# Moving layer 2's sums from GpSimd to VectorE, and s and b from the weights to the activations

## The chip, the core and the metric

The kernel runs on one core of a Trainium2 chip. A core has five engines with a queue each: TensorE (PE, with its weight load PEld), VectorE (DVE), ScalarE (ACT), GpSimd (POOL) and SyncE (SP, which here issues the DMAs). The metric is the device time of one execution in microseconds (us). Before the change it is 1638.78 us, the median of three runs (1637.3 to 1640.04).

## The reference

Linear attention feeds two dense layers. What is computed, cut to the arithmetic:

```python
kv  = einsum('bhsd,bhse->bhde', k, v)             # 8 batches, 8 heads, 576 rows, 64 wide
out = einsum('bhsd,bhde->bhse', q, kv)
x   = out / sqrt(mean(out*out, -1) + 1e-6) * g_norm   # as 4608 tokens x 512

h = x @ w_in1;  g = h * sigmoid(1.702 * h);  x = g @ w_out1     # 512 -> 2048 -> 512
h = x @ w_in2;  r = max(h, 0);  g = s * (r * r) + b;  out = g @ w_out2
```

s and b are one number each. All inputs are float32; the weights come as 64-bit words that the kernel turns into float32 itself.

## The kernel before, in words

Every float32 factor is split into a high part, rounded for TensorE, and the low rest. A product is then three matmuls: high x high, low x high, high x low. ACT makes the high part (a copy with rounding, `CAST`), DVE the low one (a subtraction).

The tokens come in 9 blocks of 512. The first three blocks of layer 1 run as plain matmuls (`mm1`, `mm2`). From there two blocks make a *couple*, and products of 2 x 2 block matrices are done with 7 block products instead of 8. Couples 0 to 2 are layer 1 (blocks 3 to 8), couples 3 to 6 are layer 2 (blocks 0 to 7), couple 7 is the *narrow* one (block 8, 256 wide). A couple has 8 *pairs*, one for 2 x 128 of the 2048 hidden columns, and a pair has 7 steps. One step of one pair is called a *slot* here.

In each slot `product` (L672) puts 6 matmuls of 512 columns on TensorE. Their right side is `xs[s, i]` (tiles `wi0` to `wi6`), one of 7 sums of the couple's input blocks, made by `y_get` (L502: load the four blocks into tiles `f0` to `f3`, and add up partial sums where layer 1 stored several), `fac_sums` (L530: three sums) and `split_x` (L544: high and low part, a fourth sum for i = 6). `after` (L768) takes the products from PSUM: ACT copies, DVE adds, ACT applies the activation. In layer 2 that is `Relu` and then `Square` (`sq`, L736).

In layer 2 two pairs make a *quad*, 14 slots. The activations of a quad, tiles `raws` e0 to e3, are the factors of 7 further products M1, M4, M7, M5, M6, M2, M3: M1, M4 and M2 use e0, e1 and e3 as they are, the other four need a sum of e's. `factor_add` (L923) makes that sum (tile `s`), on GpSimd; `factor_hi` (L945, ACT) and `factor_lo` (L953, DVE) split it (tile `fac`). `quad_unit` (L960) then puts 12 matmuls of 256 columns on TensorE, one half-product per slot, in the slots of the next quad. The three lines L979, L980 and L981 are high x high, high x low weights, and low x high, so the low part is first needed by the third matmul. M2 and M3 stay in PSUM over a couple (tile `msum`); the others are added into SBUF (tile `madd`) by DVE, or copied by ACT in a couple's first quad.

When a couple's M's are complete, `combine` (L1000) adds them to the four output blocks, per half h: five sums of SBUF tiles on GpSimd (L1012), two with PSUM on DVE, and four DMAs out.

s and b in layer 2: `prep_out` (L279) makes the 8 combinations of each weight pair and `scaled_hl` (L266) multiplies them by s while it splits them. For b, GpSimd adds all weight tiles up in `col0` (L285 to L289); `make_bias` (L865) multiplies that with b by one matmul, and the result is added when M1 and M5 of a couple are first stored (L988), and at the end of the narrow couple (L918).

What sets the order: every engine runs its queue in order. The main loop (L1520) writes, per slot, the product, what `after` does with the last one, the factors (`factors`, L1501: sums 4 slots ahead of their use, splits 2 ahead), a unit of the quad before, and then as much of the list of background tasks (`background`, L1225) as is due or fits: the kernel keeps a rough count of DVE's and ACT's time (`clock`), and lets a task go on while the larger count is under the slot's limit. Tasks are `y_get`, `fac_sums`, `split_x`, `combine`, and the conversion of layer 2's weights (`convert2`, `prepare2`), which runs during layer 1's couples. What runs on GpSimd isn't counted.

Of the kernel before, what the change touches and what calls it, by code (L numbers as in the profile page):

```python
# [44 lines left out]
SLACK2 = 0.6  # L45
# [7 lines left out]
def tile_attn_moe_moe2(  # L53
# [210 lines left out]
    wt_dram, column = {}, [None]  # L264

    def scaled_hl(dst, src, n):  # L266

        yield
        yield from spaced()
        t = rot("wst", 2, (P, 2, 2, KP), F32R)[:, 0:n]  # L270
        scalar.activation(out=t[:, :, 0, :], in_=src, func=ACTF.Copy, scale=s_sb[:, 0:1])
        yield 1
        vector.scalar_tensor_tensor(
            out=t[:, :, 1, :], in0=src, scalar=s_sb[:, 0:1], in1=t[:, :, 0, :].bitcast(F32),
            op0=ALU.mult, op1=ALU.subtract,
        )
        move(dst, t)

    def prep_out(p):  # L279

        wa, wb = (w_raw.pop((1, 1, f)) for f in (2 * p, 2 * p + 1))
        add = nc.gpsimd.tensor_tensor
        if p == 0:
            column[0] = new("col0")
            add(out=column[0], in0=wa, in1=wb, op=ALU.add)  # L285
            wt_dram.update({x: dp.tile([P, 8, 2, 2, KP], F32, name=f"wt{x}") for x in range(KF // 4)})
        else:
            add(out=column[0], in0=column[0], in1=wa, op=ALU.add)
            add(out=column[0], in0=column[0], in1=wb, op=ALU.add)  # L289
# [478 lines left out]
    def after(P_, i):  # L768
# [20 lines left out]
        elif i == 5:  # L789
            c = c_t[P_, 2]  # L790
            tt(out=c, in0=take(P_, "D"), in1=c, **add)
            sq(P_, 1)
            act(P_, 2)
        else:
            c_new(P_, 3)
            act(P_, 3, take(P_, "A"))
            g_hi(P_, 1)
            g_lo(P_, 1)
            sq(P_, 2)
            sq(P_, 3)  # L800
# [61 lines left out]
    t_t, f_t, mid_t, m_ps, m_sb, bias = {}, {}, {}, {}, {}, {}  # L862
    t_next = [0]

    def make_bias():  # L865

        b_all = kvbd[0][:, 0, :]
        o = bank("a1", "bias")
        nc.tensor.matmul(o, b_all, column[0], start=True, stop=True)
        t = new("ev1", name="bias")  # L870
        scalar.copy(t, o)
        d = new("g0", (P, KP), name="biasd")
        vector.tensor_tensor(out=d, in0=t[:, KP:2 * KP], in1=t[:, 0:KP], op=ALU.subtract)
        bias[0], bias[1], bias["all"] = t[:, 0:KP], d, t
# [36 lines left out]
    def narrow_out(t, c):  # L911
# [5 lines left out]
        for lo, hi in zip(cuts, cuts[1:]):  # L917
            vector.tensor_tensor(out=e[:, lo:hi], in0=o[:, lo:hi], in1=bias["all"][:, lo:hi], op=ALU.add)  # L918
# [4 lines left out]
    def factor_add(q_, k_):  # L923
# [3 lines left out]
        tt = nc.gpsimd.tensor_tensor  # L927
# [32 lines left out]
    def quad_unit(q_, k_, h):  # L960
# [21 lines left out]
        if not held(q_, k_):  # L982
            if first:
                a = m_sb[key] = new(ADD_PLACE[10 + h if k_ == M1 and s % 2 else 2 * k_ + h], (P, 2, KP), name="madd")
                if k_ not in (M1, M5):
                    scalar.copy(a, o)
                else:
                    more = bias[k_ == M5].rearrange("p (o d) -> p o d", o=1).to_broadcast([P, 2, KP])  # L988
                    vector.tensor_tensor(out=a, in0=o, in1=more, op=ALU.add)
# [10 lines left out]
    def combine(s, h):  # L1000
# [9 lines left out]
        def plus(k_, more, psum=False):  # L1010
# [3 lines left out]
        while (s, M6, h) not in ended:  # L1014
            yield 1
        plus(M6, m_sb[s, M1, h])
        plus(M7, m_sb[s, M6, h])
        plus(M6, m_sb[s, M5, h])
        plus(M5, m_sb[s, M7, h])
        plus(M7, m_sb[s, M4, h])  # L1020
        while (s, M2, h) not in ended:
            yield 1
        plus(M1, m_ps[s, M2, h], True)
        yield 1
        send(M1, 0, 0)
        yield 1
        send(M5, 1, 1)
        yield 1
        send(M7, 1, 0)
        while (s, M3, h) not in ended:  # L1030
            yield 1
        plus(M6, m_ps[s, M3, h], True)
# [167 lines left out]
    def plan():  # L1200
# [3 lines left out]
        for s_ in range(len(couples)):  # L1204
            n0 = n * s_
            need = []
            if s_:
                if couples[s_][0]:
                    need = [Task(y_get(s_), n0 - n + 6, n0 - n + 7)]
                need = [Task(fac_sums(s_), n0 - 14, n0 - 9, need)]  # L1210
            for i in range(7):
                if (s_, i) in split_early:
                    continue
                more = [split[s_, 1]] if (i == 6 and (s_, 1) in split) else []
                split[s_, i] = Task(split_x(s_, i), max(0, n0 - 7 + i + 1), max(0, n0 + i - (3 if i < 6 else 5)), need + more)
# [9 lines left out]
    def background(tick, slot, share):  # L1225

        limit = (tick + share) * slot
        ready = [t for t in tasks if t.ready <= tick and all(x.done for x in t.behind)]
        for t in sorted(ready, key=lambda t: due(t, tick)):
            while not t.done and t.ready <= tick and (due(t, tick) <= tick or max(clock.values()) < limit):  # L1230
                t.step(tick)

    with tc.manual_schedule():
# [286 lines left out]
        for P_, (s_, p) in enumerate(pairs):  # L1520
            lay, m, js = couples[s_]
            short = m < BT
            for i in range(7):
# [23 lines left out]
                for _ in range(2 if i == 6 else 1):  # L1547
# [9 lines left out]
                background(tick, slot, SLACK2 if lay and not short else SLACK)  # L1557
# [62 lines left out]
```

## Time and profile before

One profiled execution took 1639.39 us; its span, from the first to the last instruction, is 1637.5 us, at a mean granted TensorE clock of 0.992.

| engine | busy us | share of the span | instructions |
|---|---|---|---|
| PE (matmul) | 1579.5 | 96% | 9026 |
| PEld (weight load) | 1352.1 | 83% | 9026 |
| DVE | 984.5 | 60% | 1398 |
| ACT | 832.4 | 51% | 1430 |
| POOL | 403.3 | 25% | 208 |

The page's slices show TensorE busy at 90% or more nearly everywhere; layer 1's couples run from about 337 us, layer 2 from about 875 us, the narrow couple's own part from about 1560 us. A busy TensorE is one with matmuls in its pipe; how long it stood still, and for whom, is read from the view of waits. A wait is put down to the engine whose signal came last. Busy time of DVE or POOL is the time from an instruction's start to its end, also where it stood still inside.

### The profile page before, as it was taken

How to read it: one execution, taken by the hardware profiler on the slowest of the kernel's cores; microseconds unless marked ns; L12 is line 12 of the kernel's file. 1: busy time of each engine (PE TensorE's matmuls, PEld its weight loads, DVE VectorE, ACT ScalarE, POOL GpSimd, SP SyncE). 2: the span in 40 equal slices, each digit the busy share in tenths (PEclk: the TensorE clock that was granted, in tenths of full speed). 3: DMA queues.
4: the chain of work that ended last, by engine and by line, in shares of the span. 5: the costliest groups of instructions: out<-in, count | busy, mean ns of one | idle time of the engine just before them, and what ended most of it. 6: DMA issues, size and time to landing. Idle time of an engine off the chain costs nothing.

```text
span 1637.5 us, 23547 instructions
## 1 busy us (share of the span) xinstructions
PE 1579.5 (96%) x9026; PEld 1352.1 (83%) x9026; DVE 984.5 (60%) x1398; ACT 832.4 (51%) x1430; POOL 403.3 (25%) x208
## 2 busy tenths in 40 slices
PE   8999999999989999999889999999999999999899
PEld 7888878878877787888768898889888988899887
DVE  6777643456577667686875345754575457545732
ACT  4765633454545544554335645554555455554543
POOL 4000111101130113001440224442445244523410
PEclk9999999999999999999999999999999999999999
DMA  8678776567757766689765655575557555755584
GB/s 270 214 267 295 283 257 228 211 217 258 239 190 265 258 225 231 231 328 331 285 212 195 245 192 179 181 269 187 181 180 268 190 180 177 249 192 191 195 296 164
DMA packets 126434, 376.95 MB, mean 230 GB/s; under 512 B 12530, under 2 KB 30194, under 8 KB 118130
## 3 DMA queue, kind: packets, MB, share of 16 engines
q1 hardware_dynamic: 126178, 375.31, 66.9%
q8 instruction: 72, 1.18, 0.3%
q14 instruction: 40, 0.33, 0.1%
q10 hardware_dynamic: 144, 0.13, 0.0%
HBM read 295.70 MB, written 79.69 MB: 229 GB/s over the span
## 4 chain that ended last, share of the span: by engine, by line
PE 78%; DVE 11%; issue 4%; POOL 3%; DMA 2%; ACT 2%; SPq 0%; DVEq 0%; POOLq 0%; ACTq 0%
PE A L686 6%; PE A L687 5%; PE A L688 5%; PE m L981 4%; PE m L980 4%; PE m L979 4%; PE D L686 3%; PE D L687 3%; PE D L688 3%; DVE fac L89 3%; PE acc L626 2%; PE acc L627 2%; PE acc L628 2%; PE h L598 2%; PE h L600 2%
## 5 line engine op out<-in xcount | busy, mean ns | idle before, releaser
L981 PE MATMUL m<-wo,fac 128*128 128x256 f32 x640 | 183.0, 286 | 15.1 <-DVE fac L89 15.1
L440 POOL TENSOR_TENSOR r<-ms,mhalf 128x8 f32<-128x8 f32 x36 | 66.0, 1837 | 488.6 <-DVE ms L89 488.5
L980 PE MATMUL m<-wo,fac 128*128 128x256 f32 x640 | 181.2, 283 | 0.0
L979 PE MATMUL m<-wo,fac 128*128 128x256 f32 x640 | 180.5, 282 | 0.1
L89 DVE TENSOR_TENSOR madd<-m,madd 128x512 f32<-128x512 f32 x120 | 82.5, 687 | 101.4 <-PE m L981 101.4
L686 PE MATMUL A<-wi,xl 128*128 128x512 f32 (+1 forms) x340 | 131.5, 387 | 11.7 <-ACT ev L89 5.7
L981 PEld LDWEIGHTS m<-wo,fac 128*128 128x128 f32 x640 | 121.6, 190 | 18.3 <-DVE fac L89 17.9
L89 ACT ACTIVATE gh<-gh 128x512 f32<-128x512 f32 x72 | 45.4, 631 | 170.8 <-DVE gh L89 170.6
L687 PE MATMUL A<-wi,xl 128*128 128x512 f32 (+1 forms) x340 | 129.6, 381 | 0.0
L688 PE MATMUL A<-wi,xl 128*128 128x512 f32 (+1 forms) x340 | 128.6, 378 | 0.0
L979 PEld LDWEIGHTS m<-wo,fac 128*128 128x128 f32 x640 | 121.8, 190 | 6.9 <-issue 0.3
L980 PEld LDWEIGHTS m<-wo,fac 128*128 128x128 f32 x640 | 122.4, 191 | 5.8
L89 ACT ACTIVATE wraw<-wraw 128x512 uint32<-128x512 uint32 (+1 forms) x128 | 83.0, 648 | 80.8 <-DVE wraw L89 80.5
L89 DVE TENSOR_TENSOR fac<-s,fac 128x1024 fp32r<-128x1024 f32 x64 | 84.3, 1318 | 8.9 <-ACT fac L89 8.9
L686 PEld LDWEIGHTS A<-wi,xl 128*128 128x128 f32 x340 | 64.6, 190 | 24.0 <-ACT ev L89 6.5
L828 PE MATMUL z<-wo,wo 128*128 128x512 f32 x192 | 77.3, 403 | 5.9 <-DVE g L89 5.8
L89 DVE TENSOR_TENSOR wi<-f,wi 128x1024 fp32r<-128x1024 f32 (+1 forms) x56 | 73.9, 1327 | 9.3 <-ACT wi L89 9.3
L89 ACT ACTIVATE wi<-wi 128x512 f32<-128x512 f32 x64 | 40.5, 632 | 73.2 <-DVE wi L89 73.0
L598 PE MATMUL h<-xh,wi 128*128 128x512 f32 x192 | 76.5, 398 | 1.2 <-ACT g L89 1.2
L626 PE MATMUL acc<-gh,wo 128*128 128x512 f32 x192 | 76.7, 399 | 0.0
L627 PE MATMUL acc<-gh,wo 128*128 128x512 f32 x192 | 75.1, 391 | 1.1 <-DVE wo L89 1.1
L829 PE MATMUL z<-wo,wo 128*128 128x512 f32 x192 | 75.6, 394 | 0.0
(251 smaller groups left out, 4589.9 us busy)
## 6 DMA issues: line engine op xcount, KB each, us to landing
wo<-wt SPq DMA_DIRECT2D x127, 512.0 KB, 3.7
xl<-wi SPq DMA_DIRECT2D x42, 1024.0 KB, 6.6
wo<-wo SPq DMA_DIRECT2D x80, 512.0 KB, 5.3
xl<-wi SPq DMA_DIRECT2D x43, 768.0 KB, 5.8
xh<-wi SPq DMA_DIRECT2D x22, 1024.0 KB, 6.8
wi<-wst SPq DMA_DIRECT2D x40, 512.0 KB, 4.8
wraw<-in_w_in SPq DMA_DIRECT2D x32, 512.0 KB, 4.6
wraw<-in_w_out SPq DMA_DIRECT2D x32, 512.0 KB, 4.4
```

The costliest lines, as they stand in the source:

```text
L89: return fn(*args, **kw)
L598: nc.tensor.matmul(o, wh[:, cs], xh[:, c, :], start=(c == 0), stop=False)
L626: nc.tensor.matmul(o, wh[:, ds_], gh, start=(f == lo), stop=False)
L627: nc.tensor.matmul(o, wl[:, ds_], gh, start=False, stop=False)
L686: nc.tensor.matmul(o, wh, xh, start=(c == 0 and not more), stop=False, skip_group_check=more)
L687: nc.tensor.matmul(o, wl, xh, start=False, stop=False, skip_group_check=more)
L688: nc.tensor.matmul(o, wh, xl, start=False, stop=(c == 1), skip_group_check=more)
L828: nc.tensor.matmul(o, wh[:, cs], gh, start=begins, stop=False)
L829: nc.tensor.matmul(o, wl[:, cs], gh, start=False, stop=False)
L979: nc.tensor.matmul(o[:, c, :], hi[:, y, cs], w[:, y, 0, :], start=begins, stop=False)
L980: nc.tensor.matmul(o[:, c, :], hi[:, y, cs], w[:, y, 1, :], start=False, stop=False)
L981: nc.tensor.matmul(o[:, c, :], lo[:, y, cs], w[:, y, 0, :], start=False, stop=ends)
```

## The change

Five things change.

1. `fac_sums`, the fourth sum of `split_x`, `factor_add` and the five SBUF sums of `combine` run on DVE. For layer 2's couples after the first, `fac_sums` also makes the fourth sum, into tiles of its own, and it may start 35 slots ahead instead of 14. The adds in `y_get` and the power in `att_r` (L440) stay on GpSimd.
2. `prep_out` splits the weights unscaled (`parts_hl` for `scaled_hl`); the column sum, `make_bias` and the adds of the bias are gone. Instead `sq` is followed by a second ACT instruction on each activation tile, `Identity` with scale s and bias b.
3. `sq` of layer 2's wide couples is put on a list and issued after the slot's factors; the one of e3 is moved into the next pair's first slot, that of e1 in every second pair to the last slot of the pair.
4. In a couple's first quad M1 and M5 are copied by ACT like the others. `combine` may start 6 slots earlier, its sums are spread over slots, and the last wide couple has an order of its own (M3 copied out of PSUM by ACT first).
5. The background list has one limit for both layers (0.9 of a slot instead of 0.6 in layer 2), and in layer 2 a second one: a slot's tasks may add 500 ns to DVE's count. The units of layer 1's last pair are spread over more slots, and the two factor tile pairs change places.

```diff
-    def prep_out(p): ... add = nc.gpsimd.tensor_tensor; add(out=column[0], ...)
-        yield from scaled_hl(d[:, 0:8:7], a, 2)
+        yield from parts_hl(d[:, 0:8:7], a, 2)
...
     def fac_sums(s):
-        tt = (nc.gpsimd if s else vector).tensor_tensor
+        tt = vector.tensor_tensor
...
+        if s > first2:
+            fac[s, 6] = [new(tag, (P, couples[s][1]), name="f6") for tag in ("ev1", "g0")]
+            for c in range(2):
+                tt(out=fac[s, 6][c], in0=b21[:, c, :], in1=t2[:, c, :], op=ALU.subtract)
+                yield 1
...
+    late = []
+    def sq(P_, e, now_=False):
+        if layer(P_) and not narrow(P_) and not now_:
+            late.append((P_, e))
+        elif layer(P_):
             c = c_t[P_, e]
             scalar.activation(out=c, in_=c, func=ACTF.Square)
+            scalar.activation(out=c, in_=c, func=ACTF.Identity, scale=s_sb[:, 0:1], bias=b_sb[:, 0:1])
...
     def factor_add(q_, k_):
-        tt = nc.gpsimd.tensor_tensor
+        tt = vector.tensor_tensor
...
-                if k_ not in (M1, M5):
-                    scalar.copy(a, o)
-                else:
-                    more = bias[k_ == M5].rearrange("p (o d) -> p o d", o=1).to_broadcast([P, 2, KP])
-                    vector.tensor_tensor(out=a, in0=o, in1=more, op=ALU.add)
+                scalar.copy(a, o)
...
     def combine(s, h):
-            (vector if psum else nc.gpsimd).tensor_tensor(out=a, in0=more, in1=a, op=ALU.add)
+            vector.tensor_tensor(out=a, in0=more, in1=a, op=ALU.add)
...
                 if lay:
                     factors(*at_q)
+                if i == 0 and P_ > P2 and not narrow(P_ - 1):
+                    sq(P_ - 1, 3)
+                while late:
+                    sq(*late.pop(0), True)
...
-                background(tick, slot, SLACK2 if lay and not short else SLACK)
+                background(tick, slot, SLACK, ROOM if lay and P_ > P2 + 1 else 9999.0)
```

How the instructions stand. First GpSimd, from the last adds of `y_get` to the first sums of layer 2; `f` are the couple's input tiles, `col` the column sum, `s` the sums of activations. Before:

```order
L522 TENSOR_TENSOR f_6552<-f_6552,f_7354 128x1024
L528 TENSOR_TENSOR f_6552<-f_6552,f_7405 128x1024
L288 TENSOR_TENSOR col_3842<-col_3842,wf 128x512
L289 TENSOR_TENSOR col_3842<-col_3842,wf 128x512
L535 TENSOR_TENSOR f_7541<-f_6551,f_6549 128x1024
L537 TENSOR_TENSOR f_7542<-f_6552,f_7541 128x1024
L539 TENSOR_TENSOR f_6551<-f_6552,f_6551 128x1024
L548 TENSOR_TENSOR f_6550<-f_6550,f_7542 128x1024
L930 TENSOR_TENSOR s_7991<-wraw_7739,wst_7773 128x1024
L933 TENSOR_TENSOR s_8047<-wst_7773,wraw_7798 128x1024
```

Now the same engine, with the new file's line numbers (L503 and L509 are `y_get`):

```order
L503 TENSOR_TENSOR f_6538<-f_6538,f_7232 128x1024
L503 TENSOR_TENSOR f_6539<-f_6539,f_7286 128x1024
L503 TENSOR_TENSOR f_6539<-f_6539,f_7339 128x1024
L509 TENSOR_TENSOR f_6539<-f_6539,f_7390 128x1024
L1624 UNCONDITIONAL_BRANCH
```

Only the adds of `y_get` are left there; behind them the queue is empty to the end of the program.

Next VectorE, where couple 6 begins, from the first unit's add on; `wi` are the low parts of the couple's new right sides, `fac` the low parts of the factors, `wraw` and `wst` the activations. Before:

```order
L89 TENSOR_TENSOR madd<-m,madd 128x512
L89 TENSOR_TENSOR wi_10645<-f_10299,wi_10645 128x1024
L89 TENSOR_TENSOR wraw_10656<-B,wraw_10656 128x512
L89 TENSOR_TENSOR fac<-wi_10277,fac 128x1024
L89 TENSOR_TENSOR madd<-m,madd 128x512
L89 TENSOR_TENSOR wi_10678<-f_10298,wi_10678 128x1024
L89 TENSOR_TENSOR madd<-m,madd 128x512
L89 TENSOR_TENSOR wi_10707<-f_9343,wi_10707 128x1024
L89 TENSOR_TENSOR fac<-s_10658,fac 128x1024
```

Now:

```order
L89 TENSOR_TENSOR s_10708<-wi_10321,xh_10376 128x1024
L89 TENSOR_TENSOR madd<-m,madd 128x512
L89 TENSOR_TENSOR wi_10695<-f_9770,wi_10695 128x1024
L89 TENSOR_TENSOR wraw_10706<-B,wraw_10706 128x512
L89 TENSOR_TENSOR fac<-wi_10321,fac 128x1024
L89 TENSOR_TENSOR madd<-m,madd 128x512
L89 TENSOR_TENSOR wi_10730<-f_9332,wi_10730 128x1024
L89 TENSOR_TENSOR s_10772<-xh_10376,wi_10321 128x1024
L89 TENSOR_TENSOR madd<-m,madd 128x512
L89 TENSOR_TENSOR wi_10759<-f_9333,wi_10759 128x1024
L89 TENSOR_TENSOR wi_10761<-f_9855,wi_10761 128x512
L89 TENSOR_TENSOR fac<-s_10708,fac 128x1024
```

The two sums `s` of M7 and M5 now stand in DVE's queue, ahead of adds that free PSUM and ahead of the low parts that the next products need.

Last ScalarE at the same place, `CAST` being the high parts, `COPY` the products taken from PSUM. Before:

```order
L89 ACTIVATE xh_10333<-A 128x512
L89 ACTIVATE xh_10333<-xh_10333 128x512 x2
L89 CAST wi_10645<-f_10299 128x1024
L89 COPY wraw_10656<-A 128x512
L89 CAST fac<-wi_10277 128x1024
L89 CAST wi_10678<-f_10298 128x1024
L89 ACTIVATE wraw_10656<-wraw_10656 128x512
```

Now, with `Identity` as the rows that read `b_sb,s_sb`:

```order
L89 ACTIVATE xh_10376<-A 128x512
L89 ACTIVATE wi_10321<-wi_10321 128x512
L89 ACTIVATE wi_10321<-wi_10321,b_sb,s_sb 128x512
L89 ACTIVATE xh_10376<-xh_10376 128x512
L89 ACTIVATE xh_10376<-xh_10376,b_sb,s_sb 128x512
L89 CAST wi_10695<-f_9770 128x1024
L89 COPY wraw_10706<-A 128x512
L89 CAST fac<-wi_10321 128x1024
L89 ACTIVATE xh_10376<-xh_10376 128x512
L89 ACTIVATE xh_10376<-xh_10376,b_sb,s_sb 128x512
L89 CAST wi_10730<-f_9332 128x1024
L89 ACTIVATE wraw_10706<-wraw_10706 128x512
```

Three squares and three `Identity` stand between the last pair's final `Relu` and the high part of the new right sides; before it were two squares.

## Rows read from the trace of the kernel before

**Rows 1.** Waits of PE: who for whom: us in total, times, longest

```profile
PE m L981 <- DVE fac L89: 15.1, 14, 2.2
PE z L828 <- DVE g L89: 5.8, 4, 4.3
PE A L686 <- ACT ev L89: 5.7, 2, 4.7
PE D L686 <- DVE gh L89: 4.6, 1, 4.6
PE xtp L450 <- DVE xn L89: 4.3, 4, 2.1
PE A L686 <- DVE gh L89: 2.3, 2, 1.9
PE D L688 <- DVE wi L89: 2.0, 2, 1.4
```

**Rows 2.** Timeline in layer 2: start us, us, engine, line, what [idle before]

```profile
1242.30 2.38 POOL L933 TENSOR_TENSOR s<-wst,wraw 128x1024 f32<-128x1024 f32 x1
...
1242.39 3.37 DVE L89 TENSOR_TENSOR fac<-wraw,fac 128x1024 fp32r<-128x1024 f32 x1
...
1246.59 1.22 DVE L89 TENSOR_TENSOR fac<-s,fac 128x1024 fp32r<-128x1024 f32 x1 [0.23 <-ACT fac L89]
...
1245.82 0.39 PE L981 MATMUL m<-wo,fac 128*128 128x256 f32 x1 [1.11 <-DVE fac L89]
```

**Rows 3.** Timeline late in layer 1: GpSimd, and what TensorE waited for

```profile
780.44 1.74 POOL L288 TENSOR_TENSOR col<-col,wf 128x512 f32<-128x512 f32 x1
782.25 1.62 POOL L289 TENSOR_TENSOR col<-col,wf 128x512 f32<-128x512 f32 x1
783.84 2.81 POOL L522 TENSOR_TENSOR f<-f,f 128x1024 f32<-128x1024 f32 x1
...
844.99 2.46 POOL L537 TENSOR_TENSOR f<-f,f 128x1024 f32<-128x1024 f32 x1
...
842.69 2.51 DVE L89 TENSOR_TENSOR wc<-wf,wc 128x256 f32<-128x256 f32 x1
...
852.01 0.74 PE L686 MATMUL A<-wi,xl 128*128 128x512 f32 x1 [4.66 <-ACT ev L89]
```

**Rows 4.** Windows: us, busy of PE, PEld, DVE, ACT, POOL, granted clock, DMA share, GB/s

```profile
473.20:480.10 6.90, 5.78 (x14) 4.52 (x15) 4.46 (x9) 0.43 (x1) 0.00 (x0) 0.51 0.61 194
790.60:794.10 3.50, 3.50 (x10) 2.73 (x9) 3.50 (x3) 2.46 (x5) 2.47 (x1) 0.51 0.38 150
852.10:855.60 3.50, 3.50 (x9) 2.73 (x10) 2.56 (x4) 2.62 (x5) 0.00 (x0) 0.51 0.75 243
1039.80:1043.30 3.50, 3.50 (x13) 2.88 (x12) 3.12 (x4) 1.20 (x3) 0.23 (x1) 0.51 0.02 5
1203.60:1207.10 3.50, 3.50 (x14) 3.01 (x13) 3.20 (x4) 1.10 (x2) 0.00 (x0) 0.51 0.00 0
```

**Rows 5.** Groups by shape: busy us, mean ns of one, idle before

```profile
L89 DVE TENSOR_TENSOR f<-f,f 128x1024 f32<-128x1024 f32 x4 | 4.8, 1221 | 2.9 <-ACT f L89 2.8
L89 DVE TENSOR_TENSOR madd<-m,madd 128x512 f32<-128x512 f32 x120 | 82.5, 687 | 101.4 <-PE m L981 101.4
L1012 POOL TENSOR_TENSOR madd<-madd 128x512 f32<-128x512 f32 x40 | 61.9, 1551 | 24.3 <-DVE madd L89 21.8
L936 POOL TENSOR_TENSOR s<-s,wraw 128x1024 f32<-128x1024 f32 x8 | 19.2, 2400 | 33.7 <-DVE fac L89 33.7
L89 DVE TENSOR_TENSOR fac<-s,fac 128x1024 fp32r<-128x1024 f32 x64 | 84.3, 1318 | 8.9 <-ACT fac L89 8.9
L89 ACT CAST fac<-s 128x1024 fp32r<-128x1024 f32 x64 | 66.6, 1040 | 0.0
L89 ACT CAST wi<-wf 128x512 fp32r<-128x512 f32 x16 | 9.9, 619 | 4.7 <-DVE wf L89 4.7
L89 ACT ACTIVATE wst<-wf,s_sb 128x512 fp32r<-128x512 f32 x16 | 11.5, 719 | 0.0
```

**Rows 6.** Timeline of TensorE: the first matmul of two slots that follow each other

```profile
1249.94 0.40 PE L686 MATMUL A<-wi,xl 128*128 128x512 f32 x1
...
1252.74 0.40 PE L686 MATMUL D<-wi,xl 128*128 128x512 f32 x1
```

**Rows 7.** Windows as in rows 4: a quad within a couple, and one where a couple begins

```profile
1280.00:1320.00 40.00, 40.00 (x260) 36.42 (x259) 19.15 (x23) 20.03 (x31) 10.21 (x6) 1.00 0.58 189
1360.00:1400.00 40.00, 37.54 (x239) 33.47 (x238) 30.26 (x29) 20.78 (x30) 23.05 (x13) 1.00 0.62 206
```

More of the change, by code (lines that the diff above doesn't have):

```diff
@@ L44 @@
 SLACK = 0.9
-SLACK2 = 0.6
+ROOM = 500.0
 W_LEAST = 2.0 ** -15
@@ L791, in after @@
             tt(out=c, in0=take(P_, "D"), in1=c, **add)
-            sq(P_, 1)
+            if not (layer(P_) and not narrow(P_) and P_ % 2):
+                sq(P_, 1)
             act(P_, 2)
@@ L796, in after @@
             act(P_, 3, take(P_, "A"))
+            if layer(P_) and not narrow(P_) and P_ % 2:
+                sq(P_, 1)
             g_hi(P_, 1)
@@ L861, in tile_attn_moe_moe2 @@
     quads = [(s_, x) for s_ in range(first2, len(couples) - 1) for x in range(KF // 2 // BY)]
-    t_t, f_t, mid_t, m_ps, m_sb, bias = {}, {}, {}, {}, {}, {}
+    t_t, f_t, mid_t, m_ps, m_sb = {}, {}, {}, {}, {}
     t_next = [0]
[L865 to L874, printed above, removed]
     def load_t():
@@ L917, in narrow_out @@
         for lo, hi in zip(cuts, cuts[1:]):
-            vector.tensor_tensor(out=e[:, lo:hi], in0=o[:, lo:hi], in1=bias["all"][:, lo:hi], op=ALU.add)
+            (vector.tensor_copy if lo else scalar.copy)(e[:, lo:hi], o[:, lo:hi])
             (nc.scalar if hi < DM else nc.sync).dma_start(out=out[row:row + P, lo:hi], in_=e[:, lo:hi])
@@ L1008, in send, with plus, until @@
             nc.sync.dma_start(out=dst, in_=m_sb[s, k_, h])
-        def plus(k_, more, psum=False):
+        def plus(k_, more):
             a = m_sb[s, k_, h]
-            (vector if psum else nc.gpsimd).tensor_tensor(out=a, in0=more, in1=a, op=ALU.add)
-        while (s, M6, h) not in ended:
-            yield 1
[L1016 to L1023, printed above, removed]
+            vector.tensor_tensor(out=a, in0=more, in1=a, op=ALU.add)
+        def until(k_):
+            while (s, k_, h) not in ended:
+                yield 1
+        sums = ((M7, M6), (M6, M5), (M5, M7), (M7, M4))
+        plus(M6, m_sb[s, M1, h])
+        if s == len(couples) - 2:
+            yield from until(M2)
+            plus(M1, m_ps[s, M2, h])
+            yield from until(M3)
+            last = new(f"f{h}", (P, 2, KP), name="m3")
+            scalar.copy(last, m_ps[s, M3, h])
+            yield 4
+            send(M1, 0, 0)
+            for k_, e in sums:
+                plus(k_, m_sb[s, e, h])
+                yield 2
+            send(M5, 1, 1)
+            plus(M6, last)
+            yield 2
+            send(M7, 1, 0)
+            yield 2
+            send(M6, 0, 1)
+            return
+        yield from until(M6)
+        for k_, e in sums:
+            plus(k_, m_sb[s, e, h])
+            yield 1
+        send(M5, 1, 1)
+        yield from until(M2)
+        plus(M1, m_ps[s, M2, h])
+        yield 1
+        send(M7, 1, 0)
         yield 1
         send(M1, 0, 0)
[L1026 to L1032, printed above, removed]
+        yield from until(M3)
+        plus(M6, m_ps[s, M3, h])
         yield 1
@@ L1128, in tiles_in @@
             at((P_, 3 * e + 3), "pre", x_raw, i + e)
-    for x, slot in ((0, 2), (0, 2), (0, 5), (0, 5), (1, 3)):
+    for x, slot in ((0, 2), (0, 2), (0, 5), (0, 5), (1, 5)):
         at((P2 + x, slot), "load", load_t)
-    b_all = kvbd[0][:, 0, :]
-    at((P2, 3), "pre", lambda: scalar.activation(out=b_all, in_=ident, func=ACTF.Identity, scale=0.0, bias=b_sb[:, 0:1]))
-    at((P2 + 1, 3), "post", make_bias)
     at(n0 + 10, "load", load_q, 5 * TT)
@@ L1223, in due, with background @@
         return task.deadline() if callable(task.deadline) else task.deadline
[L1225 removed]
+    def background(tick, slot, share, room):
         limit = (tick + share) * slot
+        most = clock["dve"] + room
         ready = [t for t in tasks if t.ready <= tick and all(x.done for x in t.behind)]
         for t in sorted(ready, key=lambda t: due(t, tick)):
[L1230 removed]
+            while not t.done and t.ready <= tick and (due(t, tick) <= tick or (max(clock.values()) < limit and clock["dve"] < most)):
                 t.step(tick)
```

59 lines of the change are left out of this document (25 added, 34 removed), and 2 rows, old and new, of the table PLACES.

## The prediction

> **What bounds the kernel now.** I read the page's busy shares first: TensorE has matmuls in its pipe for 96% of the span, so time can come only from the moments in which it stands still or is clocked low. So the view of waits comes next, cut to PE's own [rows 1]. In layer 2 it waits 15.1 us for low parts of factors, mostly where a couple begins, and 2.0 us for low parts of right sides. In layer 1 it waits 5.8 us for g, 5.7 for ev, 4.6 and 2.3 for gh, 4.3 for xn: 22.7 us. Each is a tile that VectorE or ScalarE delivers late, yet both are free about half the time [rows 7]. Why late?
>
> The timeline answers. One and the same subtraction takes 3.37 us while a GpSimd sum of 2.38 us runs, and 1.22 us four microseconds later with GpSimd idle; TensorE's 1.11 us wait stands behind it [rows 2]. Late in layer 1 a 128x256 subtraction takes 2.51 us and ends at 845.2, just after GpSimd has gone over from one sum to the next (844.99), and the delay arrives at TensorE as 4.66 us [rows 3]. A VectorE instruction with two SBUF inputs thus seems to stand still until GpSimd's sum ends.
>
> Then the windows by clock: after five of the long waits the granted clock is 0.51 for 6.90 or 3.50 us, that is the lower level of 1.2 GHz [rows 4]. About half of each window is lost: 6.90 x 0.49 + 2 x 3.50 x 0.49 = 6.8 us in layer 1, 2 x 3.50 x 0.49 = 3.4 us in layer 2.
>
> **What is removed.** GpSimd loses 64 factor sums of some 2.4 us, 40 output sums of 1.55 us [rows 5], the 26 or so sums of `fac_sums` and `split_x` (2.46 us, a half for the narrow couple) and 15 column adds (1.74 and 1.62 us in the two that I show) [rows 3]. It keeps the adds of `y_get`, one of which took 2.81 us [rows 3]. In layer 2 nothing is left that could hold VectorE up.
>
> [...]
>
> **What is added, VectorE.** 64 sums at 1.22 us (the same shape and operands from SBUF: 1221 ns) are 78 us over 16 quads; 40 output sums at 0.69 us, taken like the 687 ns of `madd` with one PSUM input, are 27 us [rows 5]. A quad lasts 14 slots of 2.80 us, the distance between two slots' first matmuls [rows 6], or 39.2 us. Within a couple VectorE was busy 19.15 of 40 us [rows 7]; four sums add 4.9: about 24, far from full. Where a couple begins it was busy 30.26 [rows 7], of which about 5 was standing still beside GpSimd's 23.05 us; with 4.9 of factor sums, 3 of `fac_sums` and some output sums it comes to 30 to 34. It stays below the slot rate, but an engine that full in a queue delivers late now and then. In the narrow couple's first 11 or so slots I count 26 to 27 us of VectorE's work in about 23.5 us of matmuls: there it is the bound for a short while.
>
> **What is added, ScalarE.** Eight `Identity` per quad. The trace has none with two pointer operands: a copy is 619 ns, one with a pointer scale 719 ns [rows 5]. From below 0.62, from above 0.92 (three such steps of 100 ns); I take 0.82, the one step doubled. That is 6.6 us per quad on top of 20.03 of 40 us, or 20.78 where a couple begins [rows 7], plus two copies for M1 and M5 in a first quad: 27 to 28 of 39.2 us. At 0.92 it is 0.8 us more per quad, nothing while the queue has gaps.
>
> The first wait where that load counts is the sum of M7 in a couple's first slots, e0 - e2. Call the start of the old couple's last slot 0. The `Identity` of e2 ends at about 4.6. Before the `CAST` of the sum the ScalarE queue then holds four `CAST` at 1.04, two halves at 0.62, two copies and a `Relu` and a square at about 0.62, and one `Identity` at 0.82: 4.2 + 1.2 + 2.5 + 0.8 = 8.7 (lengths from [rows 5]; the shapes that it doesn't show are taken as the copy's). With its own 1.04 it ends at 14.3, and the subtraction of 1.32 [rows 5] at 15.6, or up to 17.0 if VectorE's queue has a low part and an add ahead of it. The third matmul of the unit needs it in the sixth slot, at 5 x 2.80 + 1.7 = 15.7. So it is 0 to 1.3 us late; I take 1.0, and 0.5 for the next sum, M5. Three boundaries at 1.5: 4.5 us, in place of about 4.4 each before. The same count inside a couple, where no right sides are split, leaves 1.1 us or more. For the narrow couple's beginning I take 5 us, what VectorE's excess of 3 us and the waits behind it give; before it was 6 of the same rows. Layer 2: 15.1 + 2.0 = 17.1 before [rows 1], 4.5 + 5 = 9.5 after, gain 7.6. Its two slow windows stood behind 2 us waits; with waits of 1 us I let them go: 3.4 more. Sum 11.0.
>
> **Layer 1.** Of 22.7 us [rows 1] I keep:
> the wait for gh of 4.6, less the two column adds that stood in its way (1.74 + 1.62 = 3.4 [rows 3]): 1.2, since the `y_get` add beside it stays;
> the other wait for gh, 2.3, beside `y_get` alone: 2.3;
> of ev's 5.7 the one early wait of 1.0, since the 4.7 is behind `fac_sums` [rows 3];
> of g's 5.8, where the longest of 4.3 is again behind `fac_sums`: 0.5;
> of xn's 4.3 two waits had a column add beside them; I take 1.25 off each, a little less than an add: 1.8.
> That is 6.8. The new sums of `fac_sums` on VectorE (12 instructions of 1.22 us, in stretches where its queue is fuller) may cost anything from 0 to 15 us; nearest is the 30.26 of 40 us [rows 7], where there is some room left, so I take 3. After: 9.8; gain 12.9. All three slow windows stood behind waits that go or shrink to about 1 us: 6.8 more. Sum 19.7.
>
> **Put at nothing:** spreading the units of layer 1's last pair, the later load, the exchanged tile pairs, ROOM: TensorE has other matmuls ready there. Cover gone, each would cost a wait like the smaller ones of rows 1, up to 2 us in either direction. The end of the kernel: one `Identity` more (0.8) in the last chain, one add less (0.7): nothing. The DMAs are the same in number and queue, and so are the matmuls but for the bias one.
>
> **Sum.** 11.0 + 19.7 = 30.7. The profiled execution took 1639.39 us (1637.5 span, 1.9 around it), 0.6 above the median of the runs. 1639.4 - 30.7 = 1608.7, and by the median 1608. Own range 1600 to 1616: the low end if boundary and narrow waits come to 1 us instead of 9.5, the high end if the slow windows of layer 2 stay and the narrow couple costs twice.
>
> **Rivals.** *All of these waits go* (chance 0.18). For it: VectorE has 5 to 15 us of room in every 40. Against it: the 23.5 us at the narrow couple, and `y_get`. Rows 1 without ev's early 1.0: 39.8 - 1.0 = 38.8, and the clock's 10.2: 49.0, so 1590.
>
> *Layer 1's end keeps its waits* (0.17). `y_get` adds stay on GpSimd, and VectorE has more instructions with two SBUF inputs beside them; the waits for gh and xn then stay whole (11.2 us) with the windows at 473 and 790, and only `fac_sums` is gone: 4.7 + 1.7 in layer 1, and 11.0 in layer 2: 17.4, so 1622. Against it: the row at 783.84 stood behind two column adds that go. [...]
>
> *Slower: ScalarE's late half sets VectorE's queue* (0.07). A sum now stands at the head of VectorE's queue and waits there for an `Identity`; behind it wait `madd` adds, which free PSUM, and low parts. Inside a couple the count above leaves 1.1 us; if ScalarE runs a slot, 2.8 us, later than I count, each such sum holds TensorE up by 1.7 us, two of four in each of some 15 quads: 51 us, against the 30.7 gained: 1659. It is slower from 2 us per quad on. Against it: ScalarE has 11 us of gaps in 39.2.
>
> *It does nothing* (0.03): the subtraction of rows 2 was long for another reason than GpSimd. Then the waits stay, 1637 to 1640. The two rows there speak against it.
>
> **How the numbers follow.** Forecast 0.55 at 1608. The range reaches to both faster rivals, 1590 to 1628: it leaves out the slower cases, those below 1590 and a part of the tails. A measurement of this kernel tells 0.2%, 3.3 us, from no change. The first three cases (0.90) are faster by more, less 0.01 for their tail; the case of nothing with that tail and some of the slower case's near side makes 0.04; slower 0.07.
>
> **What would show it.** The 128x1024 `fac` subtractions at 1.2 to 1.3 us everywhere in layer 2, none at 3.4; the factor sums on VectorE at 1.2; `Identity` at 0.8; PE's wait for `fac` 4 to 10 us instead of 15.1; no window at 0.51 in layer 2; the wait for ev down to 1.0. The wait for gh near 4.6 would bear out the second rival; many equal waits of PE for `fac` or PSUM inside quads, with VectorE idle for ACT's tile, the third. I am wrong at the root if VectorE's subtractions stay long with GpSimd idle, or if a new long wait with a slow window behind it appears where a couple begins.

## The result and the profile after

The changed kernel takes 1592.84 us, the median of four runs (1591.55 to 1593.7); the kernel before takes 1638.45 in the same comparison. The ratio is 0.972, with a 95% interval from 0.9703 to 0.9737: 45.6 us less. The forecast was 1608, 30.7 us less, with a range from 1590 to 1628. The direction and most of the mechanism were right; the size was half as large again. The profiled execution took 1592.27 us, span 1590.5, at a mean granted clock of 0.999 (0.992 before).

TensorE's waits in the changed kernel, in the columns of [rows 1] (who for whom: us in total, times, longest):

```profile
PE D L681 <- DVE gh L89: 3.2, 1, 3.2
PE m L974 <- DVE fac L89: 2.7, 6, 0.8
PE A L681 <- DMA xl<-wi: 1.7, 1, 1.7
...
PE xtp L431 <- DVE xn L89: 1.5, 4, 0.6
...
PE A L681 <- DMA xh<-wi: 1.2, 1, 1.2
...
PE z L832 <- DVE g L89: 0.7, 2, 0.6
PE A L681 <- ACT wst L89: 0.7, 1, 0.7
PE A L681 <- ACT ev L89: 0.7, 1, 0.7
```

Against [rows 1]: 15.1 for fac has become 2.7, 5.8 for g 0.7, 5.7 for ev 0.7, 4.3 for xn 1.5; the waits for wi are gone. One long wait is left, 3.2 for gh, and two for loads are new in the narrow couple.

The costs of the added work came out as taken (groups by shape: busy us, mean ns of one, idle before):

```profile
L89 DVE TENSOR_TENSOR fac<-s,fac 128x1024 fp32r<-128x1024 f32 x64 | 77.9, 1217 | 15.0 <-ACT fac L89 15.0
L89 DVE TENSOR_TENSOR fac<-wraw,fac 128x1024 fp32r<-128x1024 f32 x16 | 19.5, 1220 | 7.9 <-ACT fac L89 7.9
L89 ACT ACTIVATE xh<-xh,b_sb,s_sb 128x512 f32<-128x512 f32 x32 | 26.1, 817 | 1.1
L89 DVE TENSOR_TENSOR s<-wraw,wst 128x1024 f32<-128x1024 f32 x8 | 9.8, 1225 | 20.0 <-ACT wst L89 20.0
```

The subtraction that had a mean of 1318 ns [rows 5] is down to 1217, the `Identity` takes 817, a factor sum on VectorE 1225 instead of 2400 on GpSimd. The subtraction that is stretched in [rows 2] is down from 2232 to 1220; its row before:

```profile
L89 DVE TENSOR_TENSOR fac<-wraw,fac 128x1024 fp32r<-128x1024 f32 x16 | 35.7, 2232 | 13.1 <-ACT fac L89 13.1
```

The windows that answer to [rows 7] (us, busy of PE, PEld, DVE, ACT, POOL, granted clock, DMA share, GB/s), a quad within a couple and one where a couple begins:

```profile
1218.00:1258.00 40.00, 40.00 (x260) 36.41 (x260) 25.28 (x28) 28.38 (x43) 0.00 (x0) 1.00 0.58 192
1157.00:1197.00 40.00, 39.80 (x254) 35.96 (x254) 33.98 (x44) 29.17 (x43) 0.00 (x0) 1.00 0.63 211
```

VectorE is busier than before, 34 of 40 us where a couple begins, and TensorE still loses only 0.2 us there instead of 2.5. Busy time of VectorE was no measure of how late it delivers.

### The profile page after: what moved, and what is told of

Its sections match the earlier page's. It is cut to its first block, busy times and chain, and to the rows that moved or that the text cites. A ratio compares the mean times of both kernels' runs of the same rounds, so it can differ in the third digit from the quotient of the medians.

```text
span 1590.5 us, 23585 instructions
## 1 busy us (share of the span) xinstructions
PE 1562.8 (98%) x9024; PEld 1342.8 (84%) x9024; DVE 1010.6 (64%) x1517; ACT 954.5 (60%) x1614; POOL 99.2 (6%) x61
## 4 chain that ended last, share of the span: by engine, by line
PE 85%; DVE 6%; DMA 4%; ACT 3%; issue 1%; SPq 0%; DVEq 0%; ACTq 0%
PE A L681 6%; PE A L682 6%; PE A L683 6%; PE m L974 4%; PE m L973 4%; PE m L972 4%; PE D L681 3%; PE D L682 3%; PE D L683 3%; PE acc L621 3%; PE acc L622 3%; PE sum L832 3%; PE sum L834 3%; PE sum L833 3%; PE z L832 2%; PE acc L623 2%
## 5 line engine op out<-in xcount | busy, mean ns | idle before, releaser
L89 DVE TENSOR_TENSOR fac<-s,fac 128x1024 fp32r<-128x1024 f32 x64 | 77.9, 1217 | 15.0 <-ACT fac L89 15.0
L832 PE MATMUL z<-wo,wo 128*128 128x512 f32 x192 | 76.4, 398 | 1.2 <-DVE g L89 0.7
L833 PE MATMUL z<-wo,wo 128*128 128x512 f32 x192 | 75.0, 391 | 0.0
L623 PE MATMUL acc<-gl,wo 128*128 128x512 f32 x192 | 74.9, 390 | 0.0
L834 PE MATMUL z<-wo,wo 128*128 128x512 f32 x192 | 74.9, 390 | 0.0
```

Of the source, the lines that this page charges most:

```text
L89: return fn(*args, **kw)
L832: nc.tensor.matmul(o, wh[:, cs], gh, start=begins, stop=False)
L833: nc.tensor.matmul(o, wl[:, cs], gh, start=False, stop=False)
L834: nc.tensor.matmul(o, wh[:, cs], gl, start=False, stop=ends)
```

## The experiments

Three theories were put to the test. A: a GpSimd sum holds up VectorE. B: the sums were merely late, since GpSimd takes twice as long for one. C: the new order and limits of the queues bring the time, not the engine that does the sums.

The table has the times, and two stages from the starts of the 1536 matmuls into tile A in each trace: from the first to the 615th (column "layer 1") and from there to the 1383rd (column "layer 2"). Layer 1's couples run from the first (323.8 us before the change, not 337) to the 577th, layer 2's wide ones to the 1345th; each column reaches a pair and a half further, since the last products of the layer before run there. From the 577th to the 615th the kernel before needs 29.9 us and the changed one 27.7: the bias's two matmuls are gone, and six of layer 1's last ones now fall behind the 615th. So 2.2 us of what the column "layer 1" gains are not layer 1's. Ahead of the first A matmul the changed kernel's variants have the same work, yet it starts between 321.3 and 324.5 us: so much the start varies. Where no median is named the time is of a single run; differences are taken before rounding.

| kernel | time us | layer 1 | layer 2 |
|---|---|---|---|
| before | 1638.45 (median of 4) | 580.2 | 646.6 |
| changed | 1592.84 (median of 4) | 555.7 | 625.3 |
| pool_adds | 1620.04 | 557.3 | 653.6 |
| pool_sets | 1591.07 | 557.5 | 625.2 |
| fa_pool | 1616.77 | 559.1 | 649.4 |
| b_dve | 1616.44 | 566.5 | 639.1 |
| b_sb | 1619.37 | 561.2 | 647.6 |
| comb5 | 1601.88 | 559.7 | 632.9 |
| room_off | 1596.72 | 559.4 | 626.2 |
| fs14 | 1594.42 | 557.5 | 626.2 |
| ident2 | 1625.62 | 557.8 | 650.1 |
| y_dve | 1592.51 | 556.5 | 625.2 |
| late_send | 1596.81 | 561.8 | 625.3 |
| y_dve3 | 1584.89 (median of 5) | 550.6 | 625.3 |

**pool_adds: useless GpSimd sums beside the changed kernel's work.**

```diff
+            for y in range(2):
+                nc.gpsimd.tensor_tensor(out=d, in0=u[:, y, :], in1=v[:, y, :], op=ALU.add)
```

> The changed kernel with 128 GpSimd adds of 128x512 that nobody reads (two per factor sum, on two of the activations, 1.3 to 1.4 us each). Theory A (a GpSimd sum holds up VectorE's instructions with two SBUF inputs): the fac subtractions stretch again from 1.22 to a mean over 1.6 us, the s sums too, PE's wait for fac goes from 2.7 back to 8 to 20 us, time 1600 to 1620. Theory B (before, the sums were only late because GpSimd takes 2.4 us for one and a queue behind it): nothing waits for these adds, so VectorE's durations and the time stay, 1590 to 1596.

Layer 2 took 28.4 us more, and the time of 1620.04 us stands at the upper end of theory A's range. Nothing reads these sums, and still (waits, then a stretch of the timeline where a couple begins):

```profile
PE m L979 <- DVE fac L89: 21.7, 9, 4.7
```

```profile
1177.30 4.41 POOL L941 TENSOR_TENSOR col<-wi 128x512 f32<-128x512 f32 x2
1181.79 3.79 POOL L941 TENSOR_TENSOR col<-xh,wi 128x512 f32<-128x512 f32 x2
...
1178.23 2.32 DVE L89 TENSOR_TENSOR s<-xh,wi 128x1024 f32<-128x1024 f32 x1
1180.47 0.68 DVE L89 TENSOR_TENSOR madd<-m,madd 128x512 f32<-128x512 f32 x1
1181.08 3.39 DVE L89 TENSOR_TENSOR wi<-f,wi 128x1024 fp32r<-128x1024 f32 x2
1184.39 2.28 DVE L89 TENSOR_TENSOR fac<-s,fac 128x1024 fp32r<-128x1024 f32 x1
```

The sum of 1.22 us takes 2.32, the subtraction 2.28; the add with one input from PSUM between them keeps its 0.68. GpSimd's adds are stretched too, two take 4.41. Each stands while the other runs. VectorE has no idle time between its rows, so it waits for no buffer there. Over layer 2 the means of the stretched subtractions are 1.40 to 1.54 us, less than the 1.6 that theory A expected, and the wait for fac is a little more than its 8 to 20 us. Theory B is out as the whole story: the added sums are in nobody's chain.

**pool_sets: the same places, GpSimd only writes.**

```diff
+            nc.gpsimd.tensor_tensor(out=d[:, 0:8], in0=u[:, 1, 0:8], in1=v[:, 1, 0:8], op=ALU.add)
+            for y in range(5):
+                nc.gpsimd.memset(d, 0.0)
```

> The same places, but GpSimd writes only: an 8-column add as trigger, then five memsets of 128x512 (some 0.53 us each, 2.7 in all). Theory A in the form that two engines that read collide: VectorE at 1.22 us as without, 1590 to 1596. Theory A in the form that any work of GpSimd holds VectorE up: like the run with adds, 1600 to 1620. Theory B: 1590 to 1596.

1591.07 us, and layer 2 as in the changed kernel. GpSimd's and VectorE's groups:

```profile
L942 POOL MEMSET col<- 128x512 f32 x320 | 168.8, 527 | 18.5
```

```profile
L89 DVE TENSOR_TENSOR fac<-wi,fac 128x1024 fp32r<-128x1024 f32 x16 | 19.5, 1220 | 9.1 <-ACT fac L89 9.1
```

169 us of memsets beside the same work stretch nothing; the same subtraction has a mean of 1536 ns in pool_adds. So it is not GpSimd's activity as such; what its adds do and its memsets do not is read SBUF. The Trainium skill, "SBUF — State Buffer", section "Who interferes with whom", says so: a VectorE instruction with two SBUF inputs contends with a GpSimd instruction that reads SBUF, not with one that only writes. These two runs agree.

**fa_pool: the factor sums back on GpSimd, all else new.**

```diff
-        tt = vector.tensor_tensor        # factor_add
+        tt = nc.gpsimd.tensor_tensor
```

> The changed kernel with the 64 factor sums back on GpSimd, all else new. Theory A: fac subtractions stretched to means of 1.6 to 2.2 us where a sum runs beside them, and the sums twice as long in the chain: 15 to 35 us more in layer 2, 1607 to 1628. If the new order alone carries layer 2: 1592 to 1600.

1616.77 us; layer 2 took 24.1 us more, with these waits and durations:

```profile
PE m L974 <- DVE fac L89: 19.1, 18, 3.2
```

```profile
L89 DVE TENSOR_TENSOR fac<-wraw,fac 128x1024 fp32r<-128x1024 f32 x16 | 34.3, 2145 | 7.9 <-ACT fac L89 7.9
```

That is inside theory A's range. With the factor sums on GpSimd the rest of the change is worth nothing in layer 2: 649.4 against 646.6 before.

**b_dve: the kernel before, with its sums on VectorE and nothing else changed.**

```diff
-        tt = (nc.gpsimd if s else vector).tensor_tensor      # fac_sums; split_x, factor_add, combine alike
+        tt = vector.tensor_tensor
```

> The kernel before with one part of the change: factor sums, fac_sums, the fourth sum and combine's sums on VectorE; old order, old limits, s and b on the weights, column adds on GpSimd. Theory A: most of the gain is here, 1598 to 1612; the waits for gh and xn beside column adds and y_get stay (about 8 us), PE's wait for fac 3 to 8 us. Theory C (the new order and limits bring the time, and sums on VectorE without them would crowd its queue): 1625 to 1650, with waits for fac or PSUM inside quads.

1616.44 us, between the ranges of theories A and C. Layer 1 gained 13.7 us, layer 2 only 7.4 of 21.3. The row of waits that is new, and what stood ahead in VectorE's queue:

```profile
PE msum L981 <- DVE fac L89: 11.5, 8, 2.9
```

```profile
1202.88 3.59 DVE L89 TENSOR_TENSOR madd<-madd 128x512 f32<-128x512 f32 x5
1206.38 1.22 DVE L89 TENSOR_TENSOR fac<-xh,fac 128x1024 fp32r<-128x1024 f32 x1
```

combine's five sums stand in one row ahead of the low part of M2, which TensorE needs. On GpSimd they were in nobody's way there; on VectorE they are. So C holds in part beside A: the move alone brings a third of layer 2's gain.

**comb5: the changed kernel with the five sums in a row again, at the old due time.**

```diff
         for k_, e in sums:
             plus(k_, m_sb[s, e, h])
-            yield 1
```

> The changed kernel with the five SBUF sums of combine in one row again, at the old due time, for the wide couples but the last (still on VectorE). Theory C, as the trace of sums on VectorE in the old order suggests (rows of five sums, 3.6 us, ahead of the low part of M2 or M3, PE waits 1.6 and 0.85 at each couple start): three such places, so 5 to 9 us more than the changed kernel's 1591 to 1594, i.e. 1596 to 1602. Theory A alone (only GpSimd's sums mattered): 1591 to 1595.

Layer 2 took 7.6 us more, as C said, and the waits have the place that b_dve showed:

```profile
PE msum L974 <- DVE fac L89: 6.6, 6, 1.5
```

**room_off and fs14: two other rules of the new order undone.**

```diff
-                background(tick, slot, SLACK, ROOM if lay and P_ > P2 + 1 else 9999.0)
+                background(tick, slot, SLACK, 9999.0)
```

> The changed kernel without the second limit (a slot's background tasks may add any time to VectorE's count, up to 0.9 of a slot). Theory C: tasks crowd where a couple begins, PE's wait for fac grows from 2.7 by 2 to 8 us, 1595 to 1601. Theory A alone: 1591 to 1595.

```diff
-                need = [Task(fac_sums(s_), n0 - (14 if s_ <= first2 else 35), n0 - 9, need)]
+                need = [Task(fac_sums(s_), n0 - 14, n0 - 9, need)]
```

> The changed kernel with fac_sums released 14 slots ahead of layer 2's couples, as before, instead of 35. Theory C, by the run with sums on VectorE in the old order, where A and m waited for wi and fac 1.6 us at each couple start behind f sums in VectorE's queue: 3 to 5 us more from layer 2's start to the narrow couple (625.3 us from the 0.4 to the 0.9 point of the A products), in all 1595 to 1601. Without an effect: 625 to 626.

Theory C's sizes were missed: each is worth 0.9 us in layer 2 (626.2 against 625.3), though that is more than the 0.1 by which the runs that leave layer 2's work alone differ there. In room_off TensorE's wait for fac even fell, from 2.7 to 0.8 us, where theory C had it grow. The rest of the time of room_off is from layer 1 (below) and the start.

**b_sb: the kernel before with s and b by `Identity`, the weights split unscaled, no column sum and no bias.**

```diff
             scalar.activation(out=c, in_=c, func=ACTF.Square)
+            scalar.activation(out=c, in_=c, func=ACTF.Identity, scale=s_sb[:, 0:1], bias=b_sb[:, 0:1])
...
-            add(out=column[0], in0=column[0], in1=wa, op=ALU.add)
-            add(out=column[0], in0=column[0], in1=wb, op=ALU.add)
```

> The kernel before with the other part: no column sum and no bias, s and b by an Identity right behind each square; all other sums stay on GpSimd. Theory A: the waits beside column adds shrink (gh 4.6 to about 1.2, xn 4.3 to about 2, one slow window less, some 7 us), while each factor sum comes 0.8 to 1.6 us later onto GpSimd, which costs at the four couple starts about 1 to 2 us each: 1632 to 1642. Theory C': the Identity part is worth as much as the sums: 1610 to 1625.

1619.37 us, in the range of the rival: layer 1 gained 19.0 us (0.9 of them behind the 577th matmul), layer 2 lost 1.0. GpSimd's queue is in order, and in the kernel before a column add waits there for a weight tile of VectorE's with the sums of `fac_sums` behind it:

```profile
841.07 1.31 POOL L289 TENSOR_TENSOR col<-col,wf 128x512 f32<-128x512 f32 x1 [7.45 <-DVE wf L89]
842.33 2.58 POOL L535 TENSOR_TENSOR f<-f,f 128x1024 f32<-128x1024 f32 x1
```

These are the sums beside which the 2.51 us subtraction of [rows 3] stands. In b_sb they begin as soon as the last add of `y_get` ends:

```profile
817.11 2.41 POOL L530 TENSOR_TENSOR f<-f,f 128x1024 f32<-128x1024 f32 x1
```

The waits for ev and g fell to 1.0 and 2.7 here, with `fac_sums` still on GpSimd, and to 1.0 and 0.7 in b_dve with the column adds still there, from 5.7 and 5.8 [rows 1]. So either removal ends much of the same waits. No run takes out the column adds and leaves the scaled weights, so what each is worth in b_sb stays open.

So the gains of the parts, 13.7 and 19.0, do not add up: together they bring 18.4 to 24.5 (the nine kernels with layer 1 of the changed one need 555.7 to 561.8).

**ident2: every `Identity` twice.**

```diff
+            scalar.activation(out=c, in_=c, func=ACTF.Identity, scale=s_sb[:, 0:1], bias=b_sb[:, 0:1])
```

> The changed kernel with every Identity of layer 2 done twice (s and b are applied twice), 128 more ScalarE instructions of 0.82 us. By the rival in which ScalarE's late half sets VectorE's queue: the sums' inputs come 0.8 to 2.5 us later; where the margin is the 1.1 us that I counted inside a couple, each of some 30 sums holds PE up: 1610 to 1640. If the margin inside a couple is wider, only the four couple starts pay, 2 to 3 us each: 1598 to 1606.

Layer 2 took 24.9 us more, in the rival's range of times. Its place is another than the rival's, though. The stretch where a couple begins, and the waits:

```profile
1177.00:1217.00 40.00, 37.62 (x236) 33.58 (x235) 32.29 (x42) 32.91 (x48) 0.00 (x0) 1.00 0.61 192
```

```profile
PE m L975 <- DVE fac L89: 8.8, 9, 1.5
PE A L681 <- ACT gl L89: 5.6, 7, 1.3
PE m L973 <- ACT madd L89: 3.7, 4, 1.3
```

TensorE waits for low parts only nine times, not at 30 sums inside couples; the rest is for ScalarE's own tiles. The second `Identity` is 6.5 us more of ScalarE's work per quad (8 x 0.817) and costs 32.8 us in all, so even then the kernel is faster than before.

**late_send, y_dve and y_dve3: what is left.** First late_send, with the output DMAs of the last wide couple moved behind the last loads.

```diff
-            send(M1, 0, 0)
             for k_, e in sums:
                 plus(k_, m_sb[s, e, h])
                 yield 2
-            send(M5, 1, 1)
             plus(M6, last)
-            yield 2
-            send(M7, 1, 0)
-            yield 2
-            send(M6, 0, 1)
+            yield 18
+            for x in ((M1, 0, 0), (M5, 1, 1), (M7, 1, 0), (M6, 0, 1)):
+                send(*x)
+                yield 1
```

> The changed kernel with the eight output DMAs of the last wide couple sent some 18 slots later, when the last weights have been asked for. PE's waits for the loads of xl (1.7) and xh (1.2) in the narrow couple come from a DMA share of 0.95 to 0.98 there: if so they go, 1588 to 1591. If the loads are late for the buffers they wait for, nothing moves: 1591 to 1595.

1596.81 us: no gain, and outside both ranges. From the 1383rd A matmul to the last it took 70.2 us, the changed kernel 71.5, and kernels whose sends are unmoved 68.1 to 69.3 in other runs; the loads' waits come and go by run, so this says nothing for either expectation. But the run's layer 1 was 6.1 us longer than the changed kernel's though no instruction there differs, and that is worth more. Late in layer 1, late_send (GpSimd, VectorE, TensorE):

```profile
803.56 2.92 POOL L503 TENSOR_TENSOR f<-f,f 128x1024 f32<-128x1024 f32 x1 [3.91 <-DMA f<-y]
...
804.30 2.73 DVE L89 CUSTOM_DVE_ANT_0 wf<-wraw,wf 128x1024 uint16<-128x1024 uint16 x1
...
807.68 0.80 PE L681 MATMUL A<-wi,xl 128*128 128x512 f32 x1 [2.91 <-DVE gh L89]
```

The same place in the changed kernel:

```profile
803.68 2.59 POOL L503 TENSOR_TENSOR f<-f,f 128x1024 f32<-128x1024 f32 x1 [5.04 <-DMA f<-y]
...
803.30 0.69 DVE L89 CUSTOM_DVE_ANT_0 wf<-wraw,wf 128x1024 uint16<-128x1024 uint16 x1
```

There VectorE's instruction began 0.38 us ahead of the `y_get` add and took 0.69; here it began 0.74 behind it and took 2.73, and TensorE waited 2.9 us. The add starts when a DMA lands, so whether they meet can differ from run to run. In the changed kernel the same happened at another place (GpSimd, VectorE, TensorE):

```profile
765.98 5.67 POOL L503 TENSOR_TENSOR f<-f,f 128x1024 f32<-128x1024 f32 x2 [2.66 <-DVE wf L89]
...
766.64 2.77 DVE L89 CUSTOM_DVE_ANT_0 wf<-wraw,wf 128x1024 uint16<-128x1024 uint16 x1
769.33 2.61 DVE L89 TENSOR_TENSOR wc<-wf 128x256 f32<-128x256 f32 x1
...
774.52 0.67 PE L681 MATMUL D<-wi,xl 128*128 128x512 f32 x1 [3.18 <-DVE gh L89]
```

So the last GpSimd sums went to VectorE as well.

```diff
-                nc.gpsimd.tensor_tensor(out=got[0][0], in0=got[0][0], in1=got[0][1], op=ALU.add)
+                vector.tensor_tensor(out=got[0][0], in0=got[0][0], in1=got[0][1], op=ALU.add)
```

> The changed kernel with the 12 adds of y_get on VectorE too, which leaves GpSimd only the small powers of layer 1. Theory A: no VectorE row over 1.3 us for a fast one late in layer 1, the wait for gh of 3.2 goes and with it the slow window behind it (half of 3.5): 1586 to 1590. Rival: an add at the head of VectorE's queue waits for the DMA of its tile, and PE waits for what stands behind: 1594 to 1600.

1592.51 us: within the range of neither, between them. The stretched rows are gone, and VectorE now waits for the load, with a wait of 2.7 us of TensorE's for gh behind it:

```profile
783.77 1.23 DVE L89 TENSOR_TENSOR f<-f,f 128x1024 f32<-128x1024 f32 x1 [3.18 <-DMA f<-y]
```

In y_dve3 each add stands a slot further behind its load:

```diff
+                yield 1
+                vector.tensor_tensor(out=got[0][0], in0=got[0][0], in1=got[0][1], op=ALU.add)
                 got.pop(0)
             yield 1
-            yield 1
+            if not e:
+                yield 1
```

> The 12 adds of y_get on VectorE as in the run before, but each a slot later behind its load, so that VectorE's queue no longer waits up to 3.2 us for the DMA of its tile. Theory A: no stretched row and no wait for f<-y left at the end of layer 1, the wait for gh (2.3 to 3.3, one or two of them by run) gone with its slow window: 1585 to 1590, that is 3 to 6 us under the changed kernel's 1592.8. Rival: the adds crowd VectorE's queue as such: 1591 to 1595.

1584.89 us, the median of five runs (1584.36 to 1586.23), just under theory A's range; ratio to the kernel before 0.9679, interval 0.9663 to 0.9694, which lies below that of the changed kernel. The last 100 us of layer 1's stretch, y_dve3 first and then the changed kernel:

```profile
740.00:840.00 100.00, 100.00 (x443) 82.81 (x442) 80.41 (x127) 46.55 (x84) 0.00 (x0) 1.00 0.81 291
```

```profile
740.00:840.00 100.00, 96.82 (x421) 79.61 (x420) 71.91 (x109) 44.97 (x82) 29.98 (x12) 0.98 0.79 286
```

VectorE has 80 us of work in 100 and TensorE doesn't wait.

## Why the prediction was right, and where it was too small

*The mechanism.* That GpSimd's sums make VectorE's instructions stand still, and that TensorE's waits come from there, is shown by pool_adds, pool_sets and fa_pool. The prediction put it as "two SBUF inputs". That is too narrow: in b_sb two `TENSOR_SCALAR` with one SBUF input took 5.17 us beside the sums of `fac_sums`, against 0.88 free of them.

```profile
457.31 2.69 POOL L530 TENSOR_TENSOR f<-f,f 128x1024 f32<-128x1024 f32 x1 [5.80 <-ACT f L89]
...
457.67 5.17 DVE L89 TENSOR_SCALAR wf<-wf 128x512 f32<-128x512 f32 x2
...
468.35 0.88 DVE L89 TENSOR_SCALAR wf<-wf 128x512 f32<-128x512 f32 x2
```

The Trainium skill, "SBUF — State Buffer", section "Who interferes with whom", exempts an instruction with at most one SBUF input only outside the 2-port modes, and names `tensor_scalar` among those that can enter them; the row agrees.

*Layer 2, forecast 11.0, measured 22.6* from the 577th A matmul to the end (2.2 up to the 615th, 21.3 to the 1383rd, 0.9 lost behind it). This is the step that failed in size: "three boundaries at 1.5 ... for the narrow couple's beginning I take 5 us", 9.5 us kept. Left were 2.7 and 0.5 of waits for fac, of which the couple starts have 0.2 each and the narrow couple's beginning some 2.5. The ledger of M7 itself was close. From the start of the old couple's last slot (1156.3) the `Identity` of e2 ended at 5.0 (forecast 4.6), the `CAST` of the sum at 13.6 (14.3), and the low part came at 16.0, inside 15.6 to 17.0, 0.2 us late:

```profile
1160.45 0.82 ACT L89 ACTIVATE xh<-xh,b_sb,s_sb 128x512 f32<-128x512 f32 x1
...
1168.85 1.04 ACT L89 CAST fac<-s 128x1024 fp32r<-128x1024 f32 x1
...
1171.12 1.22 DVE L89 TENSOR_TENSOR fac<-s,fac 128x1024 fp32r<-128x1024 f32 x1
...
1172.39 0.39 PE L974 MATMUL m<-wo,fac 128*128 128x256 f32 x1 [0.20 <-DVE fac L89]
```

I took 1.0 out of 0 to 1.3 and added 0.5 for M5, which waits for nothing. (Ahead of the first high part of the new right sides stand two squares and two `Identity`, not three; the third of each comes behind it.) For the narrow couple an overload of 3 us was turned into a wait of 5, twice what was left; and the "6 of the same rows" that it was set against do not fit its own sum, since 17.1 less three times 4.4 leaves 3.9. That is 6.3 us. Another 2.3 us are waits for ScalarE's wst and g that the sum left out, of 1.5 each before, 0.7 together after; against it stand 2.9 us of waits for loads. The remaining 5.9 us, the bias's two matmuls among them, were not taken apart. That layer 2's two slow windows go was right.

What the forecast did not price at all is how combine's five sums are placed: in a row they cost 7.6 us (comb5). "Some output sums" were counted as load, and their place in the queue was worth that much.

*Layer 1, forecast 19.7, measured 22.3* up to the 577th matmul in the profiled run, 16.1 to 22.3 over the nine. The terms: g and ev at 0.7 (forecast 0.5 and 1.0), xn at 1.5 (1.8), the sums new on VectorE no visible wait (3). For gh 3.5 was kept and 3.2 measured, which is luck: what was kept were 1.2 and 2.3 at two places, what came is one wait at 774.52, with 1.4 to 2.9 us more in most other runs. Behind it stands a slow window that the forecast did not have, half of 3.5 us lost:

```profile
774.40:777.90 3.50, 3.38 (x8) 2.69 (x9) 3.16 (x6) 2.69 (x5) 0.00 (x0) 0.54 0.98 387
```

So the second rival, `y_get` against VectorE, is real, but at the length of one or two waits and not for all of layer 1's end.

*The start.* 2.2 us of the difference between the two profiled spans lie ahead of layer 1's couples, within the variation of the start; they are not from the change.

*The other rivals.* "All of these waits go" gave 1590, near the measured time, but with gh still there and only because small waits went that it did not count; y_dve3, where they do go, is at 1584.9. The slower case did not come: inside couples nothing waits at 28.4 us of ScalarE's work in 40, and in ident2, with 6.5 us more per quad, the waits cost less than the change had gained.

## What to carry to other kernels

Look at the duration of one instruction beside others of its shape: a busy engine whose instructions are stretched is being held up by a neighbour, and moving the neighbour's work onto it can make it finish sooner at a higher load. But work that is moved to an engine in somebody's chain must be spread over its queue: the move alone brought a third of layer 2's gain, and a row of five sums in the wrong place cost 7.6 us. An add that waits for a DMA should stand in an in-order queue only where the load has long landed.

## What was not expected of the hardware

A GpSimd sum is held up as well: 128x512 adds that before took 1.3 to 1.7 us came to a mean of up to 2.13 us in pool_adds, and from 1177.30 to 1186.67 in the rows above four of them and VectorE's instructions with two SBUF inputs, some 5.2 and 4.3 us alone (one of the two for wi is 128x512), took 9.4 us together: hardly more than one after the other.

```profile
L941 POOL TENSOR_TENSOR col<-wi 128x512 f32<-128x512 f32 x16 | 34.0, 2126 | 1.3
```

And the wait of 4.7 us in the middle of dense work was followed by the lower clock (0.50, 1.2 GHz) there too. There are five such stretches in pool_adds' layer 2, 20.5 us in all, so by estimate about 10 of its 28.4 us are the clock's (windows):

```profile
1186.60:1190.10 3.50, 3.38 (x13) 3.19 (x14) 3.50 (x6) 1.57 (x2) 0.00 (x0) 0.50 0.00 0
```
